# One searched order for all engines in place of corrections to a planned one: infini-attention and GELU block on one core

## Chip, core and metric

The kernel runs on one core of one Trainium2 chip. The metric is the time of one execution in device microseconds. Engines are TensorE (PE in the profile, its weight loads PEld), VectorE (DVE), ScalarE (ACT), GpSimd (POOL) and SyncE (SP), which issues nearly all transfers.

## The reference

A block of two parts on 2048 tokens of width 576 in bf16: attention over four segments of 512 tokens with 32 heads of 18, and a GELU feed-forward part of width 4608.

```python
h  = x + A(layernorm(x));  h2 = h + B(layernorm(h))
# A, per segment s (q, k, v = x@wq, x@wk, x@wv; phi(t) = t+1 if t>0 else exp(t)):
p     = softmax(q_s k_s^T * 18**-0.5 + causal mask);  a_dot = p v_s
a_mem = (phi(q_s) M) / (phi(q_s) z + 1e-6)
o     = sigmoid(beta)*a_mem + (1-sigmoid(beta))*a_dot
M, z  = M + phi(k_s)^T v_s, z + sum phi(k_s);  A = o @ wo
# B:
B(x)  = gelu(x @ w1 + b1) @ w2 + b2
```

## The kernel before

The tokens are cut into eight chunks of 256 (`c`), each of two row tiles of 128 (`tl`). Six generators describe the work of PE and, with it, what the other engines do to feed and empty it:

- `stream_P` (one for each row tile): layernorm, transposes of the normed tile (L630 by PE in the first two chunks, by a DMA transpose behind, L362), the q, k, v product (L599 and L600), its eviction into padded tiles, the transposes of q and k (L723 or L362), and phi(k) for the memory.
- `stream_A`: for each visit of up to four units the scores (L807, 16 products in 32-row tiles into the four banks of `st4`), exp (L813) into `pt`, the causal mask (L818 on POOL or L820 on DVE), the weighted values (L839, 19 columns wide, into the bank `ox`), the memory term (L863) and `finish` (L879 to L889), which frees `ox`. Exp of one visit must have read `st4` before the scores of the next can be written.
- `stream_M`: the memory update (L765).
- `stream_B`: the wo product (L599, L600), the residual, the second layernorm and its transposes, the rows with b2 to DRAM.
- `stream_F1`: x@w1 (the tail of the contraction in 64-row tiles, L1114, then L1127; in the first chunk half tiles, L1087 and L1089), eviction with the bias by DVE (L1137) or ACT (L1135), GELU on ACT (L1149). The blocks of w1 (512 KB each, L1038, and two tails, L1041) go through a few slots; a slot is loaded anew when F1 has read it.
- `stream_F2`: the w2 product (L1183), the last sum (L1187) and the output transfer (L1196; for the last row tile in two parts of 432 and 144 columns, L1194).

A planner runs these streams against a table of costs and due times (`SLACK`, changed by `PHASES`) and numbers every operation by the order in which it is made (`ops`, `made`). It also makes 53 *zero products* (L1255): products of `pq`, all zero at that time, into a free bank while PE would wait, before any F1 work. Each operation knows the operations it must wait for (`inner`) and the uses of banks it belongs to (`uses`).

What is issued is not the plan itself. `arranged()` puts the operations of each engine in the plan's order, takes out every operation named in `MOVES` and puts it behind the one named beside it, on the engine of that list; `DROP` leaves 21 zero products out, so 32 remain. `PLACE` gives each use of one of three shared banks its bank. Then a small replay of the five lists (durations of the plan, waits by `inner` and by banks) merges them into one sequence. The framework sets semaphores by that sequence, so each engine runs its own list in order and waits where an operand or a bank isn't ready. SP's transfers form one list too: a transfer that waits at its head holds those behind it.

The last lines, where the order is issued:

```python
    with tc.manual_schedule(engines={EN.PE, EN.Activation, EN.DVE, EN.Pool, EN.SP}):
        for o in arranged():
            o.issue()
```

Of the kernel before, what the change touches and what calls it, by code (L numbers as in the profile page):

```python
# [16 lines left out]
def kernel(  # L17
# [15 lines left out]
    nc = tc.nc  # L33
    P = 128
# [24 lines left out]
    def sbuf(name, shape, dt=BF16):  # L59
# [77 lines left out]
    MOVES = dict(PE=[99, -1, 84, 99, 184, 74, 95, 184, 83, 95, 182, 83, 85, 81, 206, 86, 73, 206, 97, 73, 107, 87, 90, 107, 105,  # L137
# [39 lines left out]
                 ACT=[59, -1, 55, 59, 57, 55, 101, 54, 113, 101, 124, 45, 135, 124, 130, 135, 155, 145, 168, 160, 172, 196, 224, 218, 268,  # L177
# [1168 lines left out]
```

## Time and profile before

| what | value |
|---|---|
| median of three runs | 465.13 us (464.43 to 465.53) |
| profiled execution, first to last instruction (its span; no other time of it is given) | 463.1 us |
| PE busy | 455.7 us, 98% |
| ACT, DVE, POOL busy | 324.0, 271.7, 159.6 us |
| first product on PE | 1.88 us |
| last product on PE starts | 458.8 us |
| transfers on the hardware queue | 78.80 MB |

In the rows of the profile, a group is named by line, engine, operation and tiles, with its count; a busy time is the union of the group's instructions, and matmuls overlap, so the time that a product takes PE is better read from the start of one to the start of the next. A row of the timeline gives start, length and, in brackets, how long its engine stood idle before it and what released it. Rows of the waits give the total, the number and the longest. A row of the stretches gives the length and then the busy time of PE, PEld, DVE, ACT and POOL, the clock and the DMA share.

### The profile page before, as it was taken

How to read it: one execution, taken by the hardware profiler on the slowest of the kernel's cores; microseconds unless marked ns; L12 is line 12 of the kernel's file. 1: busy time of each engine (PE TensorE's matmuls, PEld its weight loads, DVE VectorE, ACT ScalarE, POOL GpSimd, SP SyncE). 2: the span in 40 equal slices, each digit the busy share in tenths (PEclk: the TensorE clock that was granted, in tenths of full speed). 3: DMA queues.
4: the chain of work that ended last, by engine and by line, in shares of the span. 5: the costliest groups of instructions: out<-in, count | busy, mean ns of one | idle time of the engine just before them, and what ended most of it. 6: DMA issues, size and time to landing. Idle time of an engine off the chain costs nothing.

```text
span 463.1 us, 14355 instructions
## 1 busy us (share of the span) xinstructions
PE 455.7 (98%) x6081; PEld 348.5 (75%) x6081; DVE 271.7 (59%) x728; ACT 324.0 (70%) x309; POOL 159.6 (34%) x216
## 2 busy tenths in 40 slices
PE   7999999999999999999999999999999999999996
PEld 6778677677777777776777777677777788888884
DVE  6889888776875553876735656857444433312221
ACT  4997779977988788976878877668768644341520
POOL 3756254484733004565243226436241001100000
PEclk9999999999999999999999999999999999999999
DMA  8993799979696648668977475886659676564100
GB/s 227 296 337 107 163 254 170 201 185 192 182 189 141 173 152 205 148 138 180 169 198 199 123 215 127 180 232 173 161 94 252 193 199 191 101 184 148 49 28 26
DMA packets 122288, 79.71 MB, mean 172 GB/s; under 512 B 57568, under 2 KB 120432, under 8 KB 122224
## 3 DMA queue, kind: packets, MB, share of 16 engines
q1 hardware_dynamic: 122192, 78.80, 70.0%
q8 instruction: 47, 0.77, 0.7%
q14 instruction: 17, 0.14, 0.1%
q0 software_dynamic: 32, 0.01, 0.0%
HBM read 59.44 MB, written 6.49 MB: 142 GB/s over the span
## 4 chain that ended last, share of the span: by engine, by line
PE 96%; DMA 1%; ACT 0%; SPq 0%; DVE 0%; issue 0%; ACTq 0%
PE bank L1183 26%; PE bank L1127 22%; PE bank L599 13%; PE ox L839 7%; PE st L807 6%; PE late L1183 4%; PE late L1127 4%; PE bank L1114 4%; PE bank L600 3%; PE bank L1087 2%; DMA wqkv<-in_A_wk_dram 1%; PE ox L1183 1%; PE bank L863 1%; PE bank L765 1%; PE ox L1127 1%; PE bank L723 1%
## 5 line engine op out<-in xcount | busy, mean ns | idle before, releaser
L813 ACT ACTIVATE pt<-st 128x2048 bf16<-128x2048 f32 x80 | 150.2, 1878 | 47.1 <-PE st L807 42.9
L1183 PE MATMUL bank<-w_sb,hT 128*128 128x288 bf16 (+1 forms) x936 | 138.3, 288 | 0.0
L1183 PEld LDWEIGHTS <-hT 128*128 128x128 bf16 x1152 | 108.2, 98 | 28.5 <-issue 0.8
L818 POOL TENSOR_SCALAR_AFFINE_SELECT pt<-pt 128x512 bf16<-128x512 bf16 x90 | 59.2, 671 | 88.6 <-ACT pt L813 84.1
L1127 PE MATMUL bank<-xn2T,w1g 128*128 128x256 bf16 x688 | 86.7, 273 | 0.0
L1137 DVE TENSOR_TENSOR hT<-bank,b1T 128x512 bf16<-128x512 f32 x73 | 50.2, 690 | 60.6 <-PE bank L1127 60.5
L1127 PEld LDWEIGHTS <-w1g 128*128 128x128 bf16 x768 | 70.8, 98 | 16.3 <-issue 7.0
L1149 ACT ACTIVATE hT<-hT 128x1536 bf16<-128x1536 bf16 (+3 forms) x24 | 66.0, 2764 | 19.5 <-DVE hT L1137 19.3
L599 PE MATMUL bank<-wqkv,xT 128*128 128x432 bf16 (+1 forms) x268 | 57.1, 336 | 0.8 <-DMA wqkv<-in_A_wk_dram 0.7
L599 PEld LDWEIGHTS <-xT 128*128 128x128 bf16 x400 | 36.6, 97 | 19.5 <-issue 0.8
L839 PEld LDWEIGHTS <-pt 128*128 128x128 bf16 x1280 | 42.2, 96 | 5.2 <-issue 0.6
L839 PE MATMUL ox<-v_aug,pt 128*128 128x19 bf16 x1280 | 44.0, 172 | 0.3 <-DVE o_nat L885 0.3
L1135 ACT ACTIVATE hT<-bank,b1T 128x256 bf16<-128x256 f32 x72 | 30.1, 472 | 15.9 <-PE bank L1127 15.9
L807 PE MATMUL st<-QT,KT 32*128 32x128 bf16 x1280 | 32.1, 217 | 0.0
L617 POOL TENSOR_TENSOR rstd_b<-rstd_b,mhalf 128x1 f32<-128x1 f32 x16 | 9.5, 595 | 62.5 <-DVE rstd_b L612 62.5
L807 PEld LDWEIGHTS <-KT 32*128 32x128 bf16 x1280 | 18.5, 92 | 14.3 <-issue 12.7
L1127 PEld LDWEIGHTS <-wqkv 128*128 128x128 bf16 x272 | 25.7, 98 | 4.8 <-issue 1.1
L993 POOL TENSOR_TENSOR h_t<-h_t,b_bc 128x576 f32<-128x576 f32 x16 | 20.7, 1292 | 15.5 <-issue 9.3
L855 POOL TENSOR_TENSOR pq<-ek,pq 128x512 bf16<-128x512 bf16 x17 | 19.7, 1158 | 13.5 <-DVE ek L853 7.1
L1183 PE MATMUL late<-w_sb,hT 128*128 128x288 bf16 (+1 forms) x180 | 23.8, 274 | 0.0
L600 PE MATMUL bank<-wqkv,xT 65*128 65x432 bf16 (+1 forms) x67 | 22.6, 338 | 0.0
L1187 DVE TENSOR_TENSOR ot<-bank,hc 128x288 bf16<-128x288 f32 x25 | 11.3, 454 | 19.0 <-PE bank L1183 18.9
(142 smaller groups left out, 600.8 us busy)
## 6 DMA issues: line engine op xcount, KB each, us to landing
w1g<-in_B_w_dram SPq DMA_DIRECT2D x50, 512.0 KB, 4.2
wqkv<-in_B_w_dram SPq DMA_DIRECT2D x17, 512.0 KB, 4.4
w_sb<-in_B_w_dram SPq DMA_DIRECT2D x6, 864.0 KB, 7.0
hd<-h_t SPq DMA_DIRECT2D x14, 288.0 KB, 2.9
hc<-hd SPq DMA_DIRECT2D x28, 144.0 KB, 3.4
w1g<-in_B_w_dram SPq DMA_DIRECT2D x100, 32.0 KB, 3.1
x_b<-in_A_x_dram SPq DMA_DIRECT2D x18, 144.0 KB, 3.8
hT<-in_B_w_dram SPq DMA_DIRECT2D x5, 512.0 KB, 6.4
```

The lines of the kernel that those rows point to most:

```text
L599: nc.tensor.matmul(out=out_ap, lhsT=lhsT_of(slice(0, P), k), rhs=rhs_of(slice(0, P), k), start=(k == 0), stop=False)
L600: nc.tensor.matmul(out=out_ap, lhsT=lhsT_of(slice(0, KTAIL), 4), rhs=rhs_of(slice(0, KTAIL), 4), start=False, stop=True)
L807: nc.tensor.matmul(out=st4[:, i, n * P:(n + 1) * P], lhsT=KTs[(c - c % 2 + kt // 2) % 3][rows, g, (kt % 2) * P:(kt % 2 + 1) * P], rhs=QTs[ ...
L813: op("ACT", 1.88, lambda: nc.scalar.activation(out=pt[:], in_=st4[:], func=ACT.Exp, scale=scale), sk, [("pt", slot, n) for n in range(4)], ...
L818: either(("POOL", 0.64, lambda part=part: nc.gpsimd.affine_select(out=part, in_=part, pattern=[[0, 4], [1, P]], compare_op=ALU.is_ge, fill ...
L839: nc.tensor.matmul(out=oxv[:, 4 * (g % 4) + i, :], lhsT=pts[slot][:, i, n * P:(n + 1) * P], rhs=v_augs[(2 * s0 + kt) % 6][:, 4 * g + i, :] ...
L993: op("POOL", 1.29, lambda: nc.gpsimd.tensor_tensor(out=h_t[:], in0=h_t[:], in1=b2_bc[:], op=ALU.add), ["b2"], [("h", tl)], slack=SLACK["hb"])
L1127: nc.tensor.matmul(out=bank(b)[:, a * Q:(a + 1) * Q], lhsT=w1_main(wt)[:, k, (2 * (h % 2) + a) * P:(2 * (h % 2) + a + 1) * P], rhs=xn2T[c ...
L1135: nc.scalar.activation(out=hT[:, f + a, :], in_=bank(b)[:, a * Q:(a + 1) * Q], func=ACT.Identity, bias=b1T[:, f + a:f + a + 1])
L1137: either(("DVE", 0.69, lambda hT=hT, f=f, b=b: nc.vector.tensor_tensor(out=hT[:, f:f + 2, :], in0=bank(b)[:].rearrange("p (a w) -> p a w", ...
L1149: op("ACT", (f1 - f0) * Q * 0.00083 + 0.18, lambda hT=hT, f0=f0, f1=f1: nc.scalar.activation(out=hT[:, f0:f1, :], in_=hT[:, f0:f1, :], fun ...
L1183: nc.tensor.matmul(out=acc, lhsT=hT[:, q, tl * P:(tl + 1) * P], rhs=w2_sb[:, q, hs], start=(q == 0), stop=(q == NF - 1))
```

## The change

`MOVES` and `DROP` go, and with them the replay in `arranged()`. In their place stands one table `ORDER`: the whole sequence of all engines, by number; a negative entry `~i` is operation `i` on the second of the two engines that it can run on. `PLACE` is new. Four of the zero products (117, 201, 186, 116) are issued as four products of 32 columns of weights and 128 moving columns each.

```diff
-    MOVES = dict(PE=[99, -1, 84, 99, 184, 74, 95, 184, 83, 95, 182, 83, 85, 81, 206, 86, 73, 206, 97, 73, 107, 87, 90, 107, 105,
...
-    DROP = [71, 72, 73, 75, 76, 77, 81, 82, 84, 85, 92, 94, 102, 108, 118, 158, 181, 187, 202, 203, 204]
...
     gone = set()
+    QUARTERS = {117, 201, 186, 116}
...
             b = bank_slots.take()
-            op("PE", 0.213 if now < 4 else 0.11, lambda: nc.tensor.matmul(out=bank(b)[:, 0:Q], lhsT=pq[:, 0, :], rhs=pq[:, 2:4, :],
-                                                                        start=True, stop=True), ["pq"], [b])
+            quarters = len(ops) in QUARTERS
+
+            def zero_product():
+                for j in range(4 if quarters else 1):
+                    rows = slice(32 * j, 32 * j + 32) if quarters else slice(0, P)
+                    nc.tensor.matmul(out=bank(b)[rows, 0:P if quarters else Q], lhsT=pq[:, j, rows], rhs=pq[:, 2:3 if quarters else 4, :],
+                                     start=True, stop=True, **(dict(tile_position=(0, 32 * j)) if quarters else {}))
+
+            op("PE", 0.213 if now < 4 else 0.11, zero_product, ["pq"], [b])
...
     def arranged():
...
         place.update(enumerate(map(int, PLACE)))
...
+        for i in ORDER:
+            o = ops[max(i, ~i)]
+            if o.ways or o.spare:
+                o.eng, (o.dur, o.issue) = list((o.ways or o.spare).items())[i < 0]
+            yield o
```

Beside each other, the two built programs hold 2524 and 2521 operations (12164 and 12182 rows on PE, loads of weights counted): the three that go are zero products, two of which stood between the first q, k, v products. Some 180 operations change engine: among them 30 F1 evictions from ACT to DVE and 27 the other way, 17 and 16 evictions of q, k, v likewise, 29 masks from POOL to DVE and 26 the other way, 14 steps of phi(q) and 4 sums of the two attention parts from POOL to DVE, 7 and 9 the other way. Of the lists' operations, those that keep their order among each other are 576 of 1001 on PE, 173 of 387 on SP. At the start, DVE sets `pq` first instead of fourth, and POOL sets its constants ahead of the first layernorm's power (L617) instead of partly behind it; the first transposes of q (L723) stand behind the two k products instead of ahead. At the end, SP issues the wide part of the last row tile ahead of the narrow one.

More of the change, by code (lines that the diff above doesn't have):

```diff
@@ L136 @@
                         balance=143, alone=1.5, g=171, hold=-207, ln0=-104))]
-    MOVES = dict(PE=[99, -1, 84, 99, 184, 74, 95, 184, 83, 95, 182, 83, 85, 81, 206, 86, 73, 206, 97, 73, 107, 87, 90, 107, 105,
[39 rows of a table removed]
-                 ACT=[59, -1, 55, 59, 57, 55, 101, 54, 113, 101, 124, 45, 135, 124, 130, 135, 155, 145, 168, 160, 172, 196, 224, 218, 268,
[7 rows of a table removed]
-                 DVE=[14, 36, 16, 40, 24, 16, 30, 28, 41, 31, 25, 43, 17, 25, 111, 35, 39, 115, 120, 39, 19, 120, 139, 46, 140, 139, 128, 48,
[30 rows of a table removed]
-                 POOL=[20, -1, 12, 29, 22, 136, 62, 22, 23, 138, 146, 142, 173, 146, 162, 173, 197, 163, 198, 197, 237, 219, 259, 269, 285,
[9 rows of a table removed]
-                 SP=[7, 8, 6, 7, 212, 65, 361, 212, 190, 67, 231, 190, 69, 231, 272, 69, 10, 272, 64, 68, 318, 64, 11, 216, 311, 211, 233,
[19 rows of a table removed]
-    DROP = [71, 72, 73, 75, 76, 77, 81, 82, 84, 85, 92, 94, 102, 108, 118, 158, 181, 187, 202, 203, 204]
-    PLACE = ("1100212001110121120110000122121220122010120200211202021011122201021021012010210210212100201120120210"
-             "2012001201201201120200202021120102020202010211010210212012012122102012121211020220112020201202020221"
-             "0011001120001212112212121212121202021012121212210101012010101201010102001210212010100120202022012121"
-             "02020220210202121212120022102101201021")
+    ORDER = [
[112 rows of a table added]
+    PLACE = ("000000020000102200200010102021020210102021020201010112010000220021102101200120120121022102101110200111202021021021022120"
+             "110120100012100021021002121021102010102100101012010022110202021102020212002022022110212102021001210100112201110210202102"
+             "02022002112121021122101222120101101120120202002121220121001220101102012012020202210012102101202102")
     gone = set()
+    QUARTERS = {117, 201, 186, 116}
     ops = []
@@ L1273, in arranged @@
     def arranged():
-        line = {e: [o for o in sorted(ops, key=lambda o: (o.start, o.made)) if o.eng == e] for e in free_at}
-        for pairs in MOVES.values():
-            for i in pairs[0::2]:
-                line[ops[i].eng].remove(ops[i])
-        for e, pairs in MOVES.items():
-            for i, after in zip(pairs[0::2], pairs[1::2]):
-                o = ops[i]
-                if o.eng != e:
-                    o.eng = e
-                    o.dur, o.issue = (o.ways or o.spare)[e]
-                    o.end = o.start + o.dur
-                line[e].insert(line[e].index(ops[after]) + 1 if after >= 0 else 0, o)
-        place.update(enumerate(map(int, PLACE)))
-        left, held, begun = [0] * len(uses), {}, set()
-        for o in ops:
-            for u in o.uses:
-                left[u] += 1
-        def wait(o):
-            if not all(p in at for p in o.inner) or any(left[held[place[u]]] for u in o.uses if u not in begun and place[u] in held):
-                return NEVER
-            return max([0.0] + [at[p] + (0.0 if p.eng == o.eng else LAT[p.eng]) for p in o.inner])
-        order, at, free = [], {}, dict.fromkeys(line, 0.0)
-        while any(line.values()):
-            t, i, e = min((max(free[e], wait(l[0])), l[0].made, e) for e, l in line.items() if l)
-            assert t < NEVER
-            o = line[e].pop(0)
-            at[o] = free[e] = t + (0.0 if o.made in DROP else o.end - o.start if o.true is None else o.true)
-            if hasattr(o, "moves"):
-                at[o.moves] = t + o.moves.end - o.start
-            for u in o.uses:
-                begun.add(u)
-                held[place[u]] = u
-                left[u] -= 1
-            order.append(o)
-        return [o for o in order if o.made not in DROP and o.made not in gone]
+        place.update(enumerate(map(int, PLACE)))
+        for i in ORDER:
[3 more added lines that the diff above has]
+            yield o
     EN = mybir.EngineType
```

216 rows, old and new, of tables (ACT, DVE, MOVES, ORDER) are left out of this document.

## The prediction, as it was put on record

> **What bounds the kernel now.** I read the busy shares and the chain of work that ended last first, then the busy time in three stretches, the waits of PE, and the timeline of PE where a product starts later than the one ahead of it explains.
>
> ```profile
> span 463.1 us, 14355 instructions
> PE 455.7 (98%) x6081; PEld 348.5 (75%) x6081; DVE 271.7 (59%) x728; ACT 324.0 (70%) x309; POOL 159.6 (34%) x216
> ...
> PE 96%; DMA 1%; ACT 0%; SPq 0%; DVE 0%; issue 0%; ACTq 0%
> ```
> ```profile
> 0.00:9.76 9.76, 7.17 (x59) 5.54 (x60) 6.03 (x27) 5.14 (x11) 4.25 (x11) 1.00 0.79 222
> 9.76:47.40 37.64, 36.87 (x659) 28.62 (x659) 33.18 (x96) 31.06 (x33) 23.59 (x35) 1.00 0.81 244
> 47.40:459.10 411.70, 411.61 (x5366) 314.35 (x5365) 232.23 (x607) 287.81 (x265) 131.71 (x171) 1.00 0.70 166
> ```
> ```profile
> PE bank L599 <- DMA wqkv<-in_A_wk_dram: 0.7, 1, 0.7
> ```
> The chain is PE for 96%. The third stretch says more: in 411.7 us PE (first figure after the length) is idle 0.09 us. A busy PE can still be slow, so I also took every product's start-to-start time; past 47.4 us none is more than 0.02 us over its usual value for its shape, except where the row tiling changes. So an order can gain nothing there but cheaper tiling changes, and it can lose much. The other room is ahead of 47.4 us and in the last stretch behind PE.
>
> ```profile
> 19.24 0.45 PE L630 MATMUL bank<-ident,xn 128*128 128x128 bf16 x5
> 20.03 0.35 PE L839 MATMUL ox<-v_aug,pt 128*128 128x19 bf16 x8 [0.34 <-DVE o_nat L885]
> 20.43 0.54 PE L599 MATMUL bank<-wqkv,xT 128*128 128x432 bf16 x2
> ...
> 45.65 0.22 PE L1089 MATMUL bank<-xz,hT 128*128 128x128 bf16 x1
> 46.20 0.44 PE L630 MATMUL bank<-ident,xn 128*128 128x128 bf16 x5 [0.33 <-DVE MZacc L775]
> ```
> Five transposes of 128 columns take 5 x 0.056 = 0.28 us from start to start (8 take 0.45, below), yet 0.79 us pass from 19.24 to 20.03: 0.5 lost. Eight L839 products take 0.20 (16 take 0.41, below), and 0.40 pass to 20.43: 0.2 lost. From 45.65 to 46.20 0.5 of 0.55 is lost. That is 1.2; with three of 0.1 at 29.1, 29.8 and 46.7 the losses between the wait for wk and 47.4 us sum to **1.5 us**. (The second stretch shows 0.77 of them as idle time; the rest is hidden by the ends of products, which are modelled.)
>
> **The change part by part.** By the built programs both orders hold the same operations but for three zero products (2524 and 2521 operations). PE's order is rearranged throughout, some 180 evictions, masks and phi steps change engine, SP's 387 transfers are permuted, and most bank uses move.
>
> (1) Tiling changes. Both orders leave the full array almost equally often: 94 times and 93. But before, 21 of these follow a weighted product (L839) and after it 52; F2 (L1183) precedes 41 before, 17 after.
>
> ```profile
> 102.11 0.55 PE L839 MATMUL ox<-v_aug,pt 128*128 128x19 bf16 x16
> 102.52 0.65 PE L1183 MATMUL bank<-w_sb,hT 128*128 128x288 bf16 x4
> 103.00 0.55 PE L839 MATMUL ox<-v_aug,pt 128*128 128x19 bf16 x16
> 103.49 0.40 PE L807 MATMUL st<-QT,KT 32*128 32x128 bf16 x16
> ...
> 105.91 0.65 PE L1183 MATMUL bank<-w_sb,hT 128*128 128x288 bf16 x4
> 106.49 0.40 PE L807 MATMUL st<-QT,KT 32*128 32x128 bf16 x16
> ```
> Sixteen L839 take 0.41 us (102.11 to 102.52) and 0.49 when scores follow: 0.08 for the change. Four L1183 take 0.48 (102.52 to 103.00) and 0.58 when scores follow: 0.10. So 31 changes are cheaper by 0.02 each: **-0.6 us** (0.3 to 0.9 by the rounding of the rows). The Trainium skill, TensorEngine Tiling (Key Properties), says that changing the tiling mode drains the engine, and knows no price that hangs on the product ahead; by that rule alone 94 against 93 would give nothing. The trace agrees that a change costs, and shows two prices.
>
> (2) Start. The zero products (L1255) fill waits; two of the three that go stood behind the wait for wk.
>
> ```profile
> 10.99 0.27 PE L1255 MATMUL bank<-pq 128*128 128x256 bf16 x1
> 11.10 0.65 PE L599 MATMUL ox<-wqkv,xT 128*128 128x288 bf16 x4
> ...
> 11.71 0.61 PE L723 MATMUL bank<-ident,qk_pad 128*128 128x128 bf16 x8
> 12.16 0.27 PE L1255 MATMUL bank<-pq 128*128 128x256 bf16 x1
> ```
> Each costs 0.11 (10.99 to 11.10): **-0.2**. Against that, the first QT transposes (L723, x8, 0.45 from 11.71 to 12.16) ran before in the wait for wk and come after it now, behind both k products: **+0.45**. The transfers up to wk and its tail keep their places on SP, so I leave wk's landing at 9.7 us.
>
> What must stay hidden by that wait: the pow of the first layernorm (L617) now stands on POOL behind the constants that it used to precede.
>
> ```profile
> 0.79 1.53 POOL L529 MEMSET wqkv<- 1x1728 bf16 x1 [0.29 <-POOLq L1330]
> 4.26 0.57 POOL L617 TENSOR_TENSOR rstd_p<-rstd_p,mhalf 128x1 f32<-128x1 f32 x1 [0.46 <-DVE rstd_p L612]
> 12.29 0.23 POOL L529 MEMSET causal<- 128x128 bf16 x1
> 12.58 0.57 POOL L529 MEMSET wo_t<- 1x576 bf16 x1
> ```
> POOL's 4.25 busy us up to 9.76 hold two pows (1.1) and 0.2 of the prologue; the other 2.9 and causal and wo_t (0.8) now come first: from 0.79 that ends at 4.5 us, with some 0.06 of gaps each at 4.9, so pow is 0.2 to 0.6 us late. And the four zero products in quarters become 16 products of 128 columns.
>
> ```profile
> 5.67 0.27 PE L1255 MATMUL bank<-pq 128*128 128x256 bf16 x1
> ...
> 6.76 0.41 PE L599 MATMUL bank<-wqkv,xT 128*128 128x288 bf16 x2
> ```
> Ten plain ones now fill 5.67 to 6.76. Quarters are in no row: between 0.025 each (the L839 product, 0.4 for 16) and 0.11 each (the zero product, 1.8); nearest is a product of 128 columns, 0.056, 0.9 in all, plus two tiling changes at 0.1. With six plain ones 1.75, so 0.65 over the gap. Both delays together (1.25) fit: without the QT transposes (0.45) and with 0.7 of wait, PE has 1.2 of room. If a rest shows it is 0.1; at the upper end 1.0, which I keep in the range. DVE's memset of pq moves to the front of its queue, so the zero products start sooner; what follows them waits for the layernorm, so that gives nothing.
>
> (3) The waits to 47.4 us. Of the hand-overs that lost time, PE work laid between producer and consumer grows. W (L839) after the finish that frees ox: a projection pair stands between in place of one score group and transposes, 1.85 us against 0.67. First product of the next tile behind its transposes: 2.5 against 0.2. Scores behind scores at 44.5: 2.52 against 1.83. Sums of start-to-start times, all three. So I take these 1.2 us as gone. What is late next is ACT: scores (L807) need the exp before.
>
> ```profile
> 45.04 1.88 ACT L813 ACTIVATE pt<-st 128x2048 bf16<-128x2048 f32 x1 [0.92 <-PE st L807]
> 47.50 1.88 ACT L813 ACTIVATE pt<-st 128x2048 bf16<-128x2048 f32 x1 [0.58 <-PE st L807]
> ```
> Where scores waited for exp alone, exps follow at 2.46 us: the floor. The new order has six score pairs at 2.49 to 2.52 and hardly leaves ACT a gap between, where other ACT work sits. I count **0.6 us of new waits** in all (0 if every hand-over holds; 2.5 at 0.05 for each of some fifty close ones, by my estimate those in which the PE work in between exceeds the other engines' steps, at durations such as exp's 1.88, by under 0.2 us; the old order has some thirty): -1.5 + 0.6 = **-0.9**.
>
> (4) Tail.
>
> ```profile
> 457.37 0.89 PE L1183 MATMUL bank<-w_sb,hT 128*128 128x432 bf16 x4
> 458.10 0.91 PE L1183 MATMUL late<-w_sb,hT 128*128 128x144 bf16 x12
> 458.35 0.61 DVE L1187 TENSOR_TENSOR ot<-bank,h_t 128x432 bf16<-128x432 f32 x1 [5.14 <-PE bank L1183]
> 459.05 0.31 DVE L1187 TENSOR_TENSOR ot<-late,h_t 128x144 bf16<-128x144 f32 x1
> 459.38 0.81 SPq L1194 DMA_DIRECT2D out_dram<-ot  x2
> ```
> ```profile
> DMA to landing us min/median/max: 1.5/1.6/1.7
> ```
> Before, SP issues the narrow part of the last row block first, at 459.38, and the wide one behind it at 459.8; it lands 1.7 later, 461.5. After, the wide product ends one narrow group (0.25) earlier, its eviction at 458.7 and its transfer goes first; the narrow one still starts at 459.38 and lands 1.5 later, 460.9: **-0.6 us**, since nothing else is pending.
>
> **Sum**: -0.6 - 0.2 + 0.45 - 0.9 - 0.6 = -1.9 us (rounded) on the execution's span of 463.1, so 461.2. The runs shown have a median of 465.13, 2.0 above that span, spent outside it; I carry this over: **463.2 us**.
>
> **The rivals.** *(A) Small waits come back.* The new order is packed: 1.7 to 3.6 us of them, 0.03 to 0.07 at each of fifty close hand-overs. For it: ACT's floor above. Against it: the old order's third stretch, which has such hand-overs too and idles 0.09 us. Then the gains cancel: 464.3 to 466.2, middle 465.1.
>
> *(B) Late FFN weights: slower.* A w1 block can be fetched only when F1 has left its slot. In the old order at least 6.0 us of PE work lie between the last use and the next; now three blocks have 4.9, 5.3 and 5.3.
>
> ```profile
> DMA to landing us min/median/max: 3.5/4.2/9.4
> ```
> At the median nothing happens. It decides from a landing of about 6.2 us on: three waits of 1 us each, with the gain used up. At 7 us: 2.1 + 1.7 + 1.7 = 5.5, so 468.7. SP's queue adds to it, since a transfer waiting at its head holds the weights behind it.
>
> *(C) The clock.*
>
> ```profile
> 3.98 0.63 PE L1255 MATMUL bank<-pq 128*128 128x256 bf16 x2
> ...
> 4.62 0.93 PE L1255 MATMUL bank<-pq 128*128 128x256 bf16 x7
> ...
> 5.39 0.44 PE L630 MATMUL bank<-ident,xn 128*128 128x128 bf16 x5
> ```
> Seven zero products take 0.77 us from 4.62 to 5.39, 0.11 each; the three from 3.98 to 4.62 take 0.21 each: PE speeds up at 4.6 us. If quarters or the gap ahead of them lose it, the products of the next microseconds take double; what outlasts the wait for wk is some 1 us, so 464.2. The Trainium skill, TensorE: Matmul & The Clock Gate (What's actually happening), lets the clock fall after an idle window of about 3.4 us; by that rule no gap here is long enough. No run here shows a fall.
>
> That the order isn't what it says is excluded by the built program.
>
> **How the numbers follow.** Forecast 0.60 (462.4 to 464.1), A 0.22, B 0.13, C 0.05. A run of this kernel tells about 0.2% (0.9 us) from no change. Faster: forecast and part of C, 0.62. Same: most of A, 0.22. Slower: B and the top of A, 0.16. The range reaches from no new wait with the cheaper bounds, 462.3, through A to 466.3, and leaves out most of B.
>
> **What would show it.** In the new profile: L599 still waits for wk at 9.7; no PE gap over 0.2 us between 10 and 47 us; scores preceded by L839 with 0.08 for the change; the wide output transfer issued ahead of the narrow one, and 0.6 us less from PE's last product to the span's end. Waits of L1114 or L1127 for a DMA show B; many short waits for DVE or ACT show A; L599 products of 288 columns at 0.24 in place of 0.12 show C. The prediction is wrong if PE idles over 3 us past 47 us.

## The result, and the profile after

The changed kernel takes **469.36 us** (median of six runs, 467.82 to 470.15) where the kernel before takes 465.31 (464.43 to 466.11, six runs beside it): a ratio of 1.008 with an interval of 1.0063 to 1.0097. It is slower by 0.8%, 4 us above the median of before. The forecast was 463.2, the range ended at 466.3, and "slower" had a chance of 0.16. The profiled execution took 467.82, the fastest of the six, with a span of 466.1; so the trace shows 3.0 us of loss over the 463.1 of before, and a usual execution has about one more. In the changed kernel most lines stand three further down (L599 is L602, L621 is L624, L993 is L996).

The page of the changed kernel: the span, the busy times and the chain that ended last.

```profile
span 466.1 us, 14364 instructions
...
PE 456.5 (98%) x6090; PEld 352.6 (76%) x6090; DVE 273.4 (59%) x734; ACT 316.6 (68%) x301; POOL 152.4 (33%) x211
...
PE 91%; issue 2%; DVE 2%; DMA 2%; ACT 1%; POOL 1%; SPq 0%; POOLq 0%; ACTq 0%; DVEq 0%
```

PE is busy for 98% as before; this figure hides the whole difference. The chain tells it: PE 91% where it had 96%. Next the busy times by stretch (the first figure after the length is PE), cut at wk's first product, at the place that was 47.4 us before, and at the last product; and PE's waits (total, times, longest).

```profile
0.00:10.85 10.85, 7.47 (x62) 5.11 (x63) 5.06 (x22) 5.26 (x11) 5.04 (x13) 1.00 0.79 209
10.85:48.37 37.52, 35.86 (x638) 27.79 (x638) 33.34 (x91) 31.43 (x34) 24.75 (x36) 1.00 0.83 247
48.37:462.70 414.33, 412.93 (x5392) 319.63 (x5391) 234.72 (x621) 279.89 (x257) 122.65 (x162) 1.00 0.67 164
```
```profile
PE bank L633 <- DVE hT L1096: 1.2, 1, 1.2
PE bank L633 <- DVE xn L624: 0.9, 1, 0.9
PE bank L602 <- DMA wqkv<-in_A_wq_dram: 0.6, 1, 0.6
PE bank L602 <- DMA wqkv<-in_A_wk_dram: 0.6, 1, 0.6
PE bank L602 <- DVE h_t L974: 0.6, 1, 0.6
PE bank L602 <- DVE t L876: 0.4, 1, 0.4
PE late L1117 <- PE bank L1130: 0.3, 1, 0.3
PE bank L633 <- DVE o_nat L888: 0.3, 1, 0.3
```

Before, the last stretch had 0.09 us of idle PE; it has 1.40 now, and the middle one 1.66 (before 0.77). wk's first product starts at 10.85 instead of 9.76. By starts of products, less the pace of each and less what a change of tiling takes, PE loses 4.5 us behind wk at eleven places (before: 1.5): 0.49 at 35.98, 0.29 at 37.94, **1.38 at 46.94**, 0.29 and 0.14 at 82, **0.54 at 90.98**, 0.04 at 152.9, **0.73 at 193.10**, 0.14 at 260.85, 0.09 at 324.1 and **0.40 at 371.44**. Three things are behind these waits and the later start.

**A GpSimd add beside a VectorE apply.** The timelines of DVE, POOL and PE around the longest wait (start, length, line; idle time ahead in brackets):

```profile
45.76 1.96 DVE L624 TENSOR_SCALAR xn<-h_t,mv_b,rstd_b 128x576 bf16<-128x576 f32 x2
47.64 0.68 DVE L1096 TENSOR_TENSOR hT<-bank,b1T 128x512 bf16<-128x512 f32 x1
...
46.19 1.48 POOL L996 TENSOR_TENSOR h_t<-h_t,b_bc 128x576 f32<-128x576 f32 x1
...
46.94 0.22 PE L1092 MATMUL bank<-xz,hT 128*128 128x128 bf16 x1
48.37 0.44 PE L633 MATMUL bank<-ident,xn 128*128 128x128 bf16 x5 [1.21 <-DVE hT L1096]
```

The apply of layernorm b is two instructions, 0.57 and 0.31 us alone. Here the second one ends at 47.72, just after GpSimd's add of b2 (46.19 + 1.48 = 47.67). The eviction L1096 (its product had been ready since 44.91) stands behind it on DVE, and PE waits for the bank that it frees. The waits at 35.98 and 90.98 are of the same kind, beside GpSimd's product for phi(k) (34.03) and beside another add of b2 (89.76): applies of 2.0 us, ending 0.05 us after the GpSimd instruction. The Trainium skill, SBUF — State Buffer (Who interferes with whom), says that the two engines share one port pair and that a one-input VectorE instruction in a two-port mode and a GpSimd one exclude each other for a whole instruction; the three ends agree, and so do VectorE's evictions from PSUM, which take 0.67 to 0.69 us with such an add beside them or without.

**wq and wk land later.** SP's issues after wk's tail, first in the changed kernel, then in the one before; then the rows of wq's main part (KB, median us to landing), changed and before.

```profile
3.98 0.59 SPq L524 DMA_DIRECT2D x_b<-in_A_x_dram  x1
4.61 0.66 SPq L527 DMA_DIRECT2D wqkv<-in_A_wv_dram  x1
```
```profile
5.01 0.37 SPq L1053 DMA_DIRECT2D b_rows<-in_B_b_dram  x1
5.43 0.37 SPq L521 DMA_DIRECT2D x_b<-in_A_x_dram  x1
```
```profile
wqkv<-in_A_wq_dram SPq DMA_DIRECT2D x1, 576.0 KB, 6.8
```
```profile
wqkv<-in_A_wq_dram SPq DMA_DIRECT2D x1, 576.0 KB, 4.6
```

Issued at the same 1.72 us, wq takes 2.2 us longer. Before, SP stood until 5.01 for GpSimd's memset of b1's rows. That stall helped: no transfer of SP's followed wq and wk for more than a microsecond. The new order has no stall, and x_b and wv follow at once.

**Transfers issued long after their data was ready.** A store of h (hd), ready at 183.36 us, is issued at 189.49 behind a transpose that waits for GpSimd, and lands at 193.41; the addition of DVE that needs the old rows stored (L974) and then PE wait for it.

```profile
189.49 0.58 SPq L997 DMA_DIRECT2D hd<-h_t  x1
```
```profile
193.10 0.35 PE L603 MATMUL bank<-wqkv,xT 65*128 65x432 bf16 x1
194.01 0.65 PE L602 MATMUL bank<-wo_t,xT 128*128 128x288 bf16 x4 [0.56 <-DVE h_t L974]
```

The wait at 371.44 is for a transpose of xn2 that was ready at 336.01, issued at 366.97 and landed at 371.96. Those at 82 are for a transpose of o_nat that landed at 82.03, and the one at 260.85 is for a piece of w1 that landed at 260.94, as PE went on. Counting over the transfers whose landing the trace tells (first use less landing), 19 are used within 1 us of landing before, and 37 after; within 2 us 48 and 75. Counted by the semaphores that the engines' instructions wait for, it is 26 and 40, and 52 and 75: the thinning is there either way, and smaller by this count.

### The profile page after: what moved, and what is told of

The parts are those of the page before. It is cut to its first block, busy times and chain, and to the rows that moved or that the text cites. A ratio compares the mean times of both kernels' runs of the same rounds, so it can differ in the third digit from the quotient of the medians.

```text
span 466.1 us, 14364 instructions
## 1 busy us (share of the span) xinstructions
PE 456.5 (98%) x6090; PEld 352.6 (76%) x6090; DVE 273.4 (59%) x734; ACT 316.6 (68%) x301; POOL 152.4 (33%) x211
## 4 chain that ended last, share of the span: by engine, by line
PE 91%; issue 2%; DVE 2%; DMA 2%; ACT 1%; POOL 1%; SPq 0%; POOLq 0%; ACTq 0%; DVEq 0%
PE bank L1186 24%; PE bank L1130 20%; PE bank L602 12%; PE ox L842 6%; PE st L810 5%; PE late L1186 4%; PE late L1130 4%; PE bank L1117 4%; PE bank L603 3%; PE bank L1090 2%; DMA wqkv<-in_A_wk_dram 2%; DVE xn L624 1%; PE ox L1186 1%; ACT pt L816 1%; PE bank L866 1%
## 5 line engine op out<-in xcount | busy, mean ns | idle before, releaser
L1140 DVE TENSOR_TENSOR hT<-bank,b1T 128x512 bf16<-128x512 f32 x79 | 53.8, 688 | 63.1 <-PE bank L1130 62.6
L1130 PE MATMUL bank<-xn2T,w1g 128*128 128x256 bf16 x688 | 88.2, 273 | 0.0
L821 POOL TENSOR_SCALAR_AFFINE_SELECT pt<-pt 128x512 bf16<-128x512 bf16 x87 | 55.0, 644 | 91.4 <-ACT pt L816 77.7
L602 PE MATMUL bank<-wqkv,xT 128*128 128x432 bf16 (+1 forms) x268 | 57.1, 336 | 1.6 <-DMA wqkv<-in_A_wq_dram 0.6
L602 PEld LDWEIGHTS <-xT 128*128 128x128 bf16 x400 | 36.5, 97 | 22.4 <-issue 2.9
L842 PEld LDWEIGHTS <-pt 128*128 128x128 bf16 x1280 | 42.9, 96 | 4.8 <-issue 0.4
L842 PE MATMUL ox<-v_aug,pt 128*128 128x19 bf16 x1280 | 44.3, 172 | 0.0
L1138 ACT ACTIVATE hT<-bank,b1T 128x256 bf16<-128x256 f32 x60 | 25.1, 472 | 17.8 <-PE bank L1130 17.8
L996 POOL TENSOR_TENSOR h_t<-h_t,b_bc 128x576 f32<-128x576 f32 x16 | 21.3, 1332 | 9.6 <-DVE xn L624 7.8
L974 DVE TENSOR_TENSOR h_t<-bank,x_b 128x288 f32<-128x288 f32 x31 | 14.0, 456 | 16.1 <-PE bank L603 13.5
L823 DVE TENSOR_TENSOR pt<-pt,causal 128x512 bf16<-128x512 bf16 x41 | 20.1, 497 | 5.0 <-ACT pt L816 5.0
L681 ACT CAST qk_pad<-bank 128x288 bf16<-128x288 f32 (+1 forms) x27 | 12.2, 456 | 16.0 <-PE bank L603 16.0
```

What stands on the lines that cost most here:

```text
L602: nc.tensor.matmul(out=out_ap, lhsT=lhsT_of(slice(0, P), k), rhs=rhs_of(slice(0, P), k), start=(k == 0), stop=False)
L821: either(("POOL", 0.64, lambda part=part: nc.gpsimd.affine_select(out=part, in_=part, pattern=[[0, 4], [1, P]], compare_op=ALU.is_ge, fill ...
L823: ("DVE", 0.42, lambda part=part: nc.vector.tensor_tensor(out=part, in0=part, in1=causal[:].unsqueeze(1).to_broadcast([P, 4, P]), op=ALU.m ...
L842: nc.tensor.matmul(out=oxv[:, 4 * (g % 4) + i, :], lhsT=pts[slot][:, i, n * P:(n + 1) * P], rhs=v_augs[(2 * s0 + kt) % 6][:, 4 * g + i, :] ...
L996: op("POOL", 1.29, lambda: nc.gpsimd.tensor_tensor(out=h_t[:], in0=h_t[:], in1=b2_bc[:], op=ALU.add), ["b2"], [("h", tl)], slack=SLACK["hb"])
L1130: nc.tensor.matmul(out=bank(b)[:, a * Q:(a + 1) * Q], lhsT=w1_main(wt)[:, k, (2 * (h % 2) + a) * P:(2 * (h % 2) + a + 1) * P], rhs=xn2T[c ...
```

## The experiments

Twelve kernels ran, each against the kernel before on the same chip. The edits are moves in the table: `(i, at, 1)` puts operation i directly behind operation `at` in `ORDER`, 0 ahead of it. In kernels built from the changed one, lines stand three further down again (L624 is L627). Each ratio is to the kernel before, with its 95% interval; the changed kernel has 1.008 (1.0063 to 1.0097).

### Each cause by itself

*after_start: the old start.*

```diff
+    for i, at, by in ((20, 21, 0), (13, 21, 0), (12, 29, 1), (70, 12, 1), (8, 70, 1), (6, 8, 1), (7, 6, 1), (9, 7, 1), (62, 34, 1), (22, 62, 1),):
+        ORDER.remove(i)
+        ORDER.insert(ORDER.index(at) + by, i)
```

> The changed kernel with before's start put back on two queues: SP sends b1's rows ahead of the first x_b, so that it stands until GpSimd's memset of those rows, which is put back behind GpSimd's first pow. Nothing else moves. Theory (several hand-overs each come later): in the changed kernel x_b and wv are issued from 3.98 us on instead of 5.43, share the DMA engines with wq and wk, and wk's tail lands at 11.07 us instead of 10.10. With the pause back the first k product should start at 9.8 us instead of 10.85, and the span should fall by about 1.1 us from 466.1, to a ratio of 1.005 to before where the changed kernel has 1.008. Rival (wk's landing is covered by zero products and by slack later): the k product starts at 9.8 and the span stays within 0.3 us of 466.1. Rival (the new order is dear throughout, by many small waits): no change either.

Measured: 1.0076 (1.0051 to 1.0100). wk's first product starts at 9.75, as the theory said, and the time does not follow. About half of the 1.1 us is paid again at the late store:

```profile
192.00 0.35 PE L606 MATMUL bank<-wqkv,xT 65*128 65x432 bf16 x1
193.53 0.65 PE L605 MATMUL bank<-wo_t,xT 128*128 128x288 bf16 x4 [1.18 <-DVE h_t L977]
```

PE stops here at 192.00 instead of 193.10, and goes on at 193.53 instead of 194.01: this wait grew from 0.73 to 1.34 us. The rest goes at waits that the changed kernel's trace doesn't have, 0.74 at 335.3 among them. So the landing follows the theory, and the time shows no gain from it alone; the interval allows one of up to 1.4 us.

*after_port: the collisions.*

```diff
+    for i, at, by in ((271, 285, 1), (301, 271, 1), (-308, 50, 0), (454, 601, 0), (629, 609, 1), (631, 629, 1),):
...
```

> The changed kernel with six instructions put elsewhere on their own engines: the GpSimd tensor_tensor of phi(k) at 34.03 us goes behind the mask of 35.27; the b2 add of 46.19 goes directly behind it (its rows are ready at 35.36); the b2 add of 89.76 goes to 81 us; the relu and product of 89.18 and 91.20 go behind the two masks that follow them; and the eviction of 37.74 goes ahead of VectorE's gmzm product of 37.02. Theory (a VectorE instruction that reads and writes SBUF ends only when GpSimd's tensor_tensor beside it ends): the float32 apply, 0.88 us alone, took 2.0 us three times because of these GpSimd instructions, and PE waited 0.49 (at 35.98), 1.38 (at 46.94) and 0.55 us (at 90.98) beyond its pace for what was queued behind it, and 0.29 at 37.94. The three applies should take under 1.2 us each, those waits should go, and the span should fall by 2 to 2.7 us, ratio 1.002 to 1.004. Rival (the late transfers carry the loss and the PE waits only change their name): applies shorter, but the time falls by less than 0.8 us.

Measured: 1.0060 (1.0032 to 1.0088). The apply of 45.76, now at 45.92, takes 1.00 us, the other two 1.14 and 0.80, and PE's wait behind it falls from 1.38 to 0.42 us. The timeline of DVE, then of PE:

```profile
45.92 1.00 DVE L627 TENSOR_SCALAR xn<-h_t,mv_b,rstd_b 128x576 bf16<-128x576 f32 x2
46.84 0.68 DVE L1099 TENSOR_TENSOR hT<-bank,b1T 128x512 bf16<-128x512 f32 x1
...
47.57 0.44 PE L636 MATMUL bank<-ident,xn 128*128 128x128 bf16 x5 [0.25 <-DVE hT L1099]
```

But the 2 to 2.7 us expected gave about 0.9 at the median, hardly more than the rival's 0.8, and the interval overlaps that of the changed kernel. In its trace (of an execution of 470.24 us, 1.7 above its median) PE waits 1.45 us for the store at 193.85, 1.1 at 60.2 for a transpose of o_nat and 1.0 at 72.0 for w1, at places where the changed kernel's trace has 0.73 and nothing. The edit also made a wait of its own: 0.57 at 38.4, since the moved add now holds up a gmzm product ahead of QT's eviction.

*after_dma: four late transfers.*

```diff
+    for i, at, by in ((831, 874, 1), (1913, 1912, 1), (2003, 2135, 1), (2005, 2077, 1),):
...
```

> The changed kernel with four transfers put earlier on SP, each to the place where its data is ready: the store of h that was ready at 183.4 us and issued at 189.49 goes ahead of the transposes that wait for GpSimd; the two DMA transposes of the last chunk's xn2, ready at 336.0 and 348.6 and issued at 366.97 and 364.51, and the store of h ready at 349.9, go ahead of w1 pieces. Theory: PE's waits of 0.73 us at 193.10 and 0.50 us at 371.44 go, and the span falls by 1.0 to 1.3 us, ratio 1.005 to 1.006. Rival (w1's late pieces are what PE waits for, as the prediction's second rival had it): putting the transposes ahead of w1 pieces moves the wait onto w1, and the time stays or rises.

Measured: 1.0072 (1.0047 to 1.0096), 0.4 us less at the median where 1.0 to 1.3 were expected, and within noise of nothing. Both named waits are gone from the trace; others for transfers stand at 60.6 (0.4), 71.6 (0.9), 83.1 (0.4), 151.4 (0.6) and 158.0 (0.4). Those at 71.6 and 158.0 are for w1, but not at the places that the edit touched:

```profile
71.61 0.28 PE L1120 MATMUL bank<-xn2T,w1g 64*128 64x256 bf16 x1
72.51 0.39 PE L1120 MATMUL bank<-xn2T,w1g 64*128 64x256 bf16 x3 [0.62 <-DMA w1g<-in_B_w_dram]
```

Up to its first edit, at the store of 183 us, this kernel issues the changed kernel's own order, so its trace is a second look at that order. The waits behind the collisions are the same to 0.01 us (0.49, 0.29, 1.38, 0.54). Those for transfers are not: at 60.6, 71.6, 151.4 and 158.0 the changed kernel's own trace loses nothing. The piece of w1 that PE needs at 71.6 was issued at 67.5 us in both executions and landed after 5.0 us here, after 2.9 there. Which late transfer costs time differs from execution to execution, and one trace doesn't list them all; part of what "grew" or "is new" in these traces is this. The order of before has it too: in the traces of before_start and before_tail, whose edits lie elsewhere, PE loses 1.04 and 0.43 us at 80 us for a transpose of o_nat, and nothing in before's own.

*after_all: the three together.* Its edit is the three lists in one.

> The three edits of after_start, after_port and after_dma together. If the three causes are separate, their gains add: 1.1 + 2.4 + 1.2 = 4.7 us off the changed kernel's 466.1, a span of 461.4, which is 1.7 below the 463.1 of before and about what the prediction's sum gave (461.2); ratio 0.996 to 0.998. If the losses were one wait seen in three places, or new waits take their place, the sum of the three single gains is not reached and the ratio stays at 1.000 or above.

Measured: 1.0022 (1.0002 to 1.0043). The three single gains sum to 0.0032 of the ratio and together they give 0.0058. The gain of the three together is clear of noise; that it is more than the sum is not, since every single interval overlaps that of the changed kernel. That the causes hide each other is read from the traces (the store's wait that grew when PE came earlier). The sum of 4.7 us is still not reached. PE's waits in its trace:

```profile
PE bank L605 <- DMA xT<-o_nat: 2.0, 2, 1.0
...
PE bank L1133 <- DMA hT<-in_B_w_dram: 1.0, 1, 1.0
```

The waits over 0.6 us behind wk are now for transfers, three directly and one by way of VectorE (0.8 at 334.6, for an eviction that stands behind a sum which had waited for an output transfer), and none of them is one that the changed kernel's trace had pointed to.

### Margins

So the next theory: not four transfers but the whole SP line is too thin. *after_pull* puts 34 transfers earlier.

```diff
+    for i, at, by in ((302, 562, 0), (407, 405, 0), (431, 406, 0), (500, 499, 0), (507, 509, 0), (561, 554, 0), (703, 554, 0), (465, 485, 0),
...
+                      (2206, 2204, 0), (2248, 2235, 0), (2233, 2228, 0), (2360, 2334, 0), (2336, 2354, 0), (2396, 2355, 0),):
...
```

> The changed kernel with 34 transfers put earlier on SP and nothing else moved. Chosen were transfers that in its trace were first used less than 1.6 us after they landed and that were issued more than 0.6 us after their data was ready; each goes ahead of the first transfer that SP issued after that point. In the trace of the kernel before, 19 transfers are first used within 1 us of landing and 48 within 2; in the changed kernel's 37 and 75. The three single edits have shown that a wait taken away comes back in part at the next late transfer (PE's wait for the store of h at 193 us grew from 0.73 to 1.4 us when PE came there 1.1 us earlier). Theory (the new order's SP line leaves transfers too thin a margin, so that any delay is passed on to PE): the count within 1 us falls to about 20 and the time by 1.0 to 2.5 us, ratio 1.003 to 1.006. Rival (margins only look thin; GpSimd's collisions and the start carry the whole loss): time within 0.5 us of the changed kernel, ratio 1.007 to 1.009.

Measured: 1.0061 (1.0043 to 1.0080), in the theory's range at its upper end; transfers used within 1 us of landing fall from 37 to 29, not to 20, and those within 2 us from 75 to 54 (before: 48). The collisions and the start, which it doesn't touch, can hold the rest. Its interval overlaps that of the changed kernel as well, so that the time alone doesn't exclude the rival.

*after_pull3* adds the edits of after_start and after_port.

> The 34 earlier transfers together with the edits of after_start and after_port, so start, collisions and margins at once. The three edits with only four earlier transfers gave 1.0022, with waits of PE of 1.2 us each left at 59.8, 79.6 and 321.6 us for transfers that landed as PE began again. Theory: with margins mended these go too, 2 to 3.5 us less than there: ratio 0.995 to 0.998, faster than before. Rival (each wait removed is paid again elsewhere, since the DMA engines are the limit): 1.001 to 1.003 as there.

Measured: 0.9995 (0.9978 to 1.0012). The whole loss is gone, 0.0085 of the ratio, where the single edits of start, collisions and margins sum to 0.0043 (each of them uncertain by about 0.003). The theory had it faster than before, and that isn't shown; its trace still shows 2 us of waits.

```profile
PE bank L605 <- DMA xT<-o_nat: 0.7, 2, 0.4
PE bank L605 <- DMA wqkv<-in_A_wk_dram: 0.6, 1, 0.6
PE bank L605 <- DVE QT L732: 0.4, 1, 0.4
PE bank L636 <- DVE hT L1099: 0.3, 1, 0.3
```

*after_pull_port* is after_pull3 without the start's edit.

> The changed kernel with the 34 earlier transfers and the collisions' edit, but with its own start. Alone these two gave 1.0061 and 1.0060, together with before's start 0.9995. Theory (start, collisions and margins each carry a part, and a part pays in full only when the next late hand-over is gone too): without the start's edit the first k product is back at 10.4 to 11.3 us, 1.1 to 2 us later than the 9.27 of after_pull3, and the time is 1 us above that kernel's, ratio 1.0015 to 1.003. Rival (the start is covered later and carries nothing): ratio 0.999 to 1.0005, as after_pull3.

Measured: 1.0024 (1.0010 to 1.0039), as the theory said: 0.0029 more than after_pull3, with wk's first product at 10.44 instead of 9.27. So the start, which showed no gain alone, is worth some 1.3 us once the rest is mended (0.3 to 2.4 by the two intervals).

### The same causes put into the kernel before

*before_start* moves b1's rows behind the second x_b, so that SP does not stand.

```diff
+        for i, a, by in ((70, 9, 1),):
+            order.remove(ops[i])
+            order.insert(order.index(ops[a]) + by, ops[i])
```

> The kernel before with one transfer moved: b1's rows go behind the second x_b on SP, so that SP does not stand until 5.01 us and issues x_b and wv from 3.98 on, as in the changed kernel. Theory of the start: wq and wk land later because the later transfers now share the DMA engines with them; the first k product starts at 10.6 to 11 us instead of 9.76, and the span rises by about 1 us, ratio 1.002. Rival (landing differs by chance between executions, not by this order): first k product within 0.3 us of 9.76, ratio 1.000.

Measured: 1.0009 (0.9997 to 1.0022); wk's first product at 10.29, wk's tail landed at 10.49. The landing moves as the theory says, but less, and the time does not tell the two theories apart. Nor does wk's first product: it starts at 10.00 and 10.41 in before_tail and before_port, which keep the pause. The landings of all fourteen traces do: with SP's pause wq's tail lands at 6.64 to 7.41 us (eight kernels) and wk's tail at 8.94 to 10.10; without it at 8.13 to 9.59 and 10.49 to 11.55 (six kernels).

*before_port* lays two of GpSimd's adds beside applies.

```diff
+        for i, a, by in ((301, 322, 1), (302, 555, 1), (454, 547, 1),):
...
```

> The kernel before with two of GpSimd's b2 adds put later, so that they lie beside VectorE's float32 applies as in the changed kernel: that of 40.03 us behind the pow of 44.44 (and the store of h that needs it behind the next x load), that of 78.44 behind the mask of 85.81. Theory of the collisions: the applies of 44.66 (1.12 us) and 85.89 (1.09 us) end only when the adds end and take 1.9 and 1.8 us; PE waits 0.5 to 1.4 us more for the instructions queued behind them, ratio 1.001 to 1.004. Rival: VectorE has room behind those applies, the PE start times behind them are unchanged, ratio 1.000.

Measured: 1.0003 (0.9994 to 1.0013). In the trace, that of the slowest of its twelve runs, both collisions are there. Behind the first PE's wait at 46.3 grows from 0.50 to 1.14 us; behind the second, an apply of 2.06 us at 87.98, PE doesn't wait, as the rival had it:

```profile
45.32 1.76 DVE L621 TENSOR_SCALAR xn<-h_t,mv_b,rstd_b 128x576 bf16<-128x576 f32 x2
...
46.31 0.22 PE L1089 MATMUL bank<-xz,hT 128*128 128x128 bf16 x1
47.50 0.44 PE L630 MATMUL bank<-ident,xn 128*128 128x128 bf16 x5 [0.97 <-DVE MZacc L775]
```

The time shows nothing of these 0.64 us with certainty: its interval reaches from -0.3 to +0.6. The mechanism is shown by the rows, its price in this kernel is not.

*before_tail* takes over the changed kernel's end alone.

```diff
+        for i, a, by in ((2545, 2536, 1), (2538, 2550, 0),):
...
```

> The kernel before with the end of the changed one: the last wide product of the output is issued ahead of the last group of narrow ones, and its transfer is the first of the last two on SP. The prediction put 0.6 us on this; the two traces have 2.73 us from the last product's start to the last landing before and 2.17 after. Theory: 0.4 to 0.7 us less, ratio 0.9985 to 0.9992. Rival (the end of the changed kernel is shorter for another reason, such as less traffic beside it): ratio 1.000 within 0.0005.

Measured: 0.9979 (0.9967 to 0.9991), 1.0 us (0.4 to 1.5). From the last product's start to the end of the span its trace has 3.66 us, before 4.34. The tail holds what the prediction put on it, and perhaps more.

### A version that beats both

*after_best* mends four waits of after_pull3 at their cause.

```diff
+    for i, at, by in (
...
+                      (300, 328, 1), (299, 300, 1), (50, 299, 1), (52, 377, 1), (703, 554, 1), (647, 703, 1), (405, 431, 1), (407, 405, 1),):
...
```

> After_pull3 with the four waits that its trace still shows attacked where the trace puts their cause: gmzm's product and the two copies to xz, which waited for GpSimd's add at 35.4, go behind the additions to h_t of 38 us (PE waited 0.57 at 36.4); the gmzm product ahead of the apply of 43.96 goes behind the eviction that the apply held up (0.42 at 45.1); w1 pieces go behind the transpose of o_nat of 53.68 (0.49 at 58.3); and two x loads go behind the transpose of o_nat of 77.17 (0.61 at 79.3). Theory: these 2.1 us leave the span, ratio 0.995 to 0.997, and the order's own gains (wide tiling, zero products, tail; 1.9 us in the prediction's sum) come out as time at last. Rival (PE goes from one late hand-over to the next, and what is taken away at one is paid at another): ratio 0.999 to 1.000.

Measured: 0.9981 (0.9963 to 0.9999), span 462.8, between the two theories and within noise of after_pull3. The four waits are gone or under 0.15 us; the larger waits in its trace are new ones, one of the edit's own making (xz) and three for w1, the transfers of the prediction's second rival.

```profile
PE bank L1120 <- DMA w1g<-in_B_w_dram: 1.2, 3, 0.7
...
PE bank L1095 <- DVE xz L993: 0.7, 1, 0.7
```

*after_best2* mends these.

```diff
...
+                      (300, 309, 1), (299, 300, 1), (50, 328, 1), (52, 377, 1), (703, 554, 1), (647, 703, 1), (405, 431, 1), (407, 405, 1),
+                      (1430, 1595, 0), (1596, 1595, 1), (1764, 1827, 0), (1763, 1764, 0), (2231, 2258, 0), (2247, 2245, 1),):
...
```

> After_best with the waits that its own trace shows mended: the two copies to xz, which its edit had put too late (PE waited 0.82 us at 37.4 for them), go directly behind the eviction of QT that they had held up; and six transfers around the three places where PE waited for w1 (0.39 us at 256.2, 0.93 at 300.9, 0.62 at 379.9) change places: pieces of w1 that were ready 2 to 17 us before their issue go earlier, and a transpose of KT that lay beside one of them goes ahead of it. Theory (each wait is real time once nothing else is late): up to 2.7 us less than after_best's 0.9981, ratio 0.993 to 0.996. Rival (PE runs into the next late transfer): ratio 0.997 to 0.9985, with new waits for transfers of 0.5 us and more at places where after_best has none.

Measured: **0.9950** (0.9935 to 0.9964), median 463.82 us beside 466.20 of before: faster than both kernels. Its profiled execution (465.68 us) is the slowest of its six runs, so its trace should show more waits than a usual one:

```profile
PE bank L605 <- DMA wqkv<-in_A_wk_dram: 1.2, 1, 1.2
PE bank L1133 <- DMA w1g<-in_B_w_dram: 1.0, 1, 1.0
PE bank L605 <- DMA xT<-o_nat: 1.0, 1, 1.0
PE bank L771 <- POOL phik_pad L752: 0.7, 1, 0.7
```

The ratio lies in the theory's range: the mended waits are gone from the trace, and the time fell by 0.0031, 1.4 us of the 2.7 hoped for. The rival keeps something too: in this execution PE waits about 1 us for a transfer at 72.0 and again at 319.4, where after_best's trace has nothing.

## Why the prediction was wrong

The steps that held. **Tiling changes**: in the changed kernel 44 changes from the weighted product to scores cost 0.078 us each, against the 0.08 of point 1, and those behind F2 0.096 against 0.10; a pair of its rows shows the first (sixteen L842 from 105.76 to 106.17, 0.41; 104.79 to 105.27, 0.48 when scores follow).

```profile
104.79 0.55 PE L842 MATMUL ox<-v_aug,pt 128*128 128x19 bf16 x16
105.27 0.40 PE L810 MATMUL st<-QT,KT 32*128 32x128 bf16 x16
...
105.76 0.55 PE L842 MATMUL ox<-v_aug,pt 128*128 128x19 bf16 x16
106.17 1.63 PE L1186 MATMUL bank<-w_sb,hT 128*128 128x288 bf16 x12
```

**The tail** went further than its term: from the last product's start (462.70) to the end of the span are 3.40 us, before 4.34, so -0.9 where -0.6 stood, and before_tail shows it as time. **The hand-overs** named in point 3 lose nothing any more. **The late pow and the quarters** cost nothing, as point 2 said, though both were mis-sized and the wait that hides them is the new one for wq: the pow starts 1.1 us later (5.34 instead of 4.26) and not 0.2 to 0.6, and the sixteen quarter products take 0.34 us (6.80 to 7.14) and not 0.9.

The steps that failed:

- Point 2, "The transfers up to wk and its tail keep their places on SP, so I leave wk's landing at 9.7 us." Their places and issue times are the same; what is issued behind them is not. The term was 0 and measured +1.1 us. The prediction's own quoted rows had POOL's constants moving, and it looked at the pow alone, not at what SP's next transfer waited for.
- Point 3, "I count 0.6 us of new waits in all". 4.5 us were there. This is the step that decides: with -0.6 for tiling, -0.9 for the tail, +1.1 for the start, +0.25 for point 2's other items (taken from the prediction, not tried) and +3.0 for the waits (4.5 less the 1.5 of before), the sum is +2.85 against the +3.0 in the traces. That is one execution of each kernel, the changed kernel's fastest; the second look at its order, in after_dma, shows 2.3 us more of waits for transfers up to 183 us. The rule used was to compare the PE work between a producer and its consumer with the other engines' steps at their usual durations. It cannot see a step that doubles because another engine runs beside it (apply 0.88 to 2.0 us), an eviction queued behind that step, or a transfer that is ready early and issued late.
- Rival A had the sign right and the form wrong: it expected some fifty waits of 0.03 to 0.07 us, and gave ACT's exp as a reason; there were eleven, of up to 1.38, none of them for exp. Rival B, late w1 blocks, is 0.14 us of the changed kernel's trace but 1.3 us of the same order in after_dma's (71.6 and 158.0), and waits for w1 come up in the kernels built from it (0.39, 0.93 and 0.62 us in after_best). Its figure, 468.7, lies nearest to the measured 469.36; since w1 is only a part of the loss, that is luck. Rival C had its signature, q products of 288 columns at 0.24 us, in one trace (after_pull at 8.9 us).
- The prediction's test "PE idles over 3 us past 47 us" was not met either: some 2.4 of the 4.5 us lie past it. It looked for the loss in the wrong stretch.
- The 2.0 us added for time outside the span was 1.7 in the changed kernel's run (467.82 beside 466.1). The term set a median beside the span of one execution.

And an order's gain is a sum only while nothing else is late. Once the start, the collisions and the thin transfers were mended, the new order is 0.5% faster than the old, 2.3 us at these runs' ratio, and the forecast's sum was 1.9. Of the 2.3, before_tail shows 1.0 (0.4 to 1.5) that two moves give the old order as well, and the old order's own waits were not mended; that the tiling term is a part of the rest was not tried by itself.

## What to carry to other kernels

When an order of many engines is changed, look not only at what each instruction waits for but at what runs beside it: a GpSimd instruction beside a VectorE one from SBUF to SBUF, and the transfers issued behind the one that PE needs. For each transfer take first use less landing, and issue less readiness; transfers that are both late in issue and thin in margin are where time will be lost, also where a given trace shows no wait. One cause mended can show no gain until the next late transfer is mended too, so try them together before a cause is dismissed, and read more than one trace of an order before a wait is called new.

## What the runs showed of the hardware

A transfer issued first isn't served alone: 648 KB of wq, issued by 2.75 us, land about 2 us later when others follow from 3.98 us instead of 5.01 on the same queue (before_start, where one transfer moved, is among the late ones). The Trainium skill, DMA: Bandwidth & Descriptors (Queues, rings and completion order), says that each DMA engine consumes descriptors in ring order, and that a later one may still finish its write before an earlier one; by the ring order alone the later x_b and wv should not have held up wq so long, and the landings of fourteen traces say that they did (6.64 to 7.41 against 8.13 to 9.59).

Not every VectorE instruction takes longer beside a GpSimd product or add. Over the traces of before and after, applies, mask products (L823, before L820, 0.42 us alone, up to 1.05) and phi products (L859, 0.41 alone, 1.41 beside the b2 add) can; evictions from PSUM, the additions to h_t (0.46) and bn_stats do not.

The moment at which PE's products go to twice the pace differs between executions: seven zero products from 3.78 us on take 1.05 us in after_dma and 1.70 in after_pull, whose first instructions are the same, and in after_pull the q products at 8.87 still take 0.24 each. First after_dma, then after_pull:

```profile
3.78 1.05 PE L1266 MATMUL bank<-pq 128*128 128x256 bf16 x7
```
```profile
3.77 1.70 PE L1266 MATMUL bank<-pq 128*128 128x256 bf16 x7
```
```profile
8.87 1.09 PE L605 MATMUL bank<-wqkv,xT 128*128 128x288 bf16 x4
```

The profile shows a granted clock of 1.00 throughout, so the reason stays open.
